# Four PSUM banks as tiles of one bank each, in a windowed attention with a maxout layer computed by a Strassen scheme

## The chip, the cores and the metric

The kernel runs on one core of a Trainium2 chip. The metric is the device time of one execution in microseconds (us): the median of several runs, and beside it one execution that the hardware profiler recorded. TensorE is called PE here, its weight loads PEld, VectorE DVE, ScalarE ACT, GpSimd POOL, and SyncE, which issues the DMAs, SP.

## What is computed

Eight batches of eight heads attend over 576 positions, each query to 32 keys: the 32 before it, or every fourth of the last 128. The result, 4608 rows of 512, goes through a layer that takes the maximum of three products and multiplies it by a fourth matrix. All is float32.

```python
# attention: B, H, S, D = 8, 8, 576, 64; window 32, dilation 4
mask_plain = (rel >= 0) & (rel < window)
mask_dil = (rel >= 0) & (rel < window * dilation) & (rel % dilation == 0)
scores = np.where(masks, scale * q @ k.T, -1e9)
attn = np.exp(scores - scores.max(-1)); attn /= attn.sum(-1) + 1e-09
x = (attn @ v).transpose(0, 2, 1, 3).reshape(4608, 512)
# maxout: w1, w2, w3 are 512 x 768, w_out is 768 x 512
h = np.maximum(np.maximum(x @ w1, x @ w2), x @ w3)
out = h @ w_out
```

## The kernel before

Every float32 operand of the layer is split into a high and a low part that PE multiplies fast, so one product is three: high by high, high by low, low by high.

The rows are worked on in tiles: three plain ones of 512 rows (tiles 0 to 2, `plain`, line 1193) and four of 768 rows by a Strassen scheme (tiles 3 to 6, `fast`, line 1292). In a plain tile each of the 18 weight blocks gives 12 matmuls of 512 columns (L1227) into one bank, and DVE or ACT takes the running maximum into `hf`. In a Strassen tile the weights are taken in nine items of two blocks each, and an item is seven products P1 to P7 of six matmuls of 384 columns (L1396) instead of eight. P1, P6, P7 and P4 accumulate one after the other in the bank `top`, P5 and P3 in `mid`, P2 in `side`. Between them the bank is read: `copied` (line 1409) copies it to SBUF as `s1`, `s5` or `u2`, and `result` (line 1415) adds bank and copy and takes the maximum into `hf`. The products stand in an order of their own, `order` (lines 1377 to 1381): items follow each other by 7, so that P4 of an item comes after P1 and P5 of the next.

At the end of a tile, `down_part` (line 1118) multiplies `hf` by the fourth matrix in blocks of 128 rows: ACT casts the high part `h`, POOL or DVE makes the low part, PE runs 18 matmuls (L1149) into one bank, ACT copies it to `o`, and SP stores `o`. In a Strassen tile the first block is opened before the last P4.

Attention runs beside this in units of one batch and two heads. The first eight (`early`, line 565) hold scores in two neighbouring banks (`bb`) and values in two single banks and one pair of neighbouring ones; their result goes to `xs`, the input of tiles 0 and 1. The later ones (`attention`, line 837) use four single banks and write `raw`, from which the Strassen tiles make their operands.

For the Strassen weights, `sums_of` (line 1049) makes sums and differences of the weight blocks on POOL and DVE, splits them, and stores them to DRAM (`kept_a`, `kept_b`; L1085); each Strassen tile loads them again (L1357).

PSUM has eight banks. Banks 0 to 5 are three tiles `pair_0` to `pair_2` of two banks each (line 394), banks 6 and 7 the tiles `ffn_0` and `ffn_1`. `ALLOWED` (line 397) says which a buffer may take: early attention and the weights' scratch `cp` any of 0 to 5, later attention 0 to 3, a plain tile 6 and 7, a Strassen tile 4 to 7.

All work is given as steps with costs, dependences and buffers to a planner (`Plan`, line 117), which simulates the engines, picks for each engine the next step by due time, gives out the banks (`banks`, line 175: the bank that is free earliest, and of those one whose neighbour is in use), and so fixes each engine's order of instructions. Semaphores between the engines are set afterwards by the framework from the tiles that the instructions read and write. The layer's own products are chained by `prev` and keep their order; attention goes between them. PE runs filler matmuls (L1572) until the first layer product.

Of the kernel before, what the change touches and what calls it, by code (L numbers as in the profile page):

```python
# [8 lines left out]
F32 = mybir.dt.float32  # L9
# [321 lines left out]
def tile_dilated_window_attention__then__maxout_ffn(  # L331
# [16 lines left out]
    ps = ctx.enter_context(tc.tile_pool(name="ps", bufs=1, space=bass.MemoryType.PSUM))  # L348
# [21 lines left out]
    plan = Plan()  # L370
# [20 lines left out]
    KEPT["sa"] = [flat[0][:, 10752 + 2048 * i : 12800 + 2048 * i] for i in range(3)]  # L391
    KEPT["sb"] = [flat[0][:, 16896:18432], *(flat[1][:, 1536 * i : 1536 * i + 1536] for i in range(3))]

    pairs = [ps.tile([128, 2, 512], F32, name=f"pair_{i}") for i in range(3)]
    BANKS = [x[:, i] for x in pairs for i in range(2)]
    BANKS += [ps.tile([128, 512], F32, name=f"ffn_{i}") for i in range(2)]
    ALLOWED = {"b": range(6), "late": range(4), "ffn": (6, 7), "fast": range(4, 8)}

    def buf(tag, name, shape=None, dtype=None):
        if tag == "bb":  # L400
            b = Buf([x for x in pairs for _ in range(2)], "b", 8, None, None, name)
            b.width, b.allowed = 2, range(0, 6, 2)
            return b
        if tag in ALLOWED:
            b = Buf(BANKS, "b", 8, None, None, name)
            b.allowed = ALLOWED[tag]
            return b
        if tag in KEPT:
            return Buf(KEPT[tag], tag, len(KEPT[tag]), None, None, name)
        n, sh, dt = SIZES[tag]  # L410
        return Buf(big if tag in ("h", "wd") else work, tag, n, shape or sh, dtype or dt, name)

    def copy(eng, dst, src):
        if eng == "act":
            nc.scalar.copy(dst, src)  # L415
        elif eng == "pool":
            nc.gpsimd.tensor_scalar(dst, src, 1.0, 1.0, ALU.mult, ALU.mult)
        else:
            nc.vector.tensor_copy(dst, src)
# [22 lines left out]
    def tt(eng, dst, a, b, op):  # L442
        (nc.vector if eng == "dve" else nc.gpsimd).tensor_tensor(dst, a, b, op=op)  # L443


    def act(n, psum=True):
        return (0.155 if psum else 0.195) + 0.00084 * n

    def dve(n):
        return 0.15 + 0.00105 * n  # L450
# [4 lines left out]
    def pool1(n):  # L455
        return 0.22 + 0.00093 * n

    def pool(n):
        return 0.13 + 0.00238 * n
# [3 lines left out]
    DOWN = [*((f, 0, DM) for f in range(NF - 1)), (NF - 1, 0, 256), (NF - 1, 256, 256)]  # L463
    NW = NWU + len(DOWN)
    wdn = [buf("wd", f"wdn{f}") for f in range(NF)]

    def weight(j, before):

        up = j < NWU
        f, n0, n = (None, 0, 512) if up else DOWN[j - NWU]  # L470
        tag = "wd" if n == 512 else "o"
        st = buf(tag, f"st{j}", [128, 2 * n], F32)
        res = [] if up else [wdn[f]]

        def part(z):
            if up:
                return wup[:, j, z]
            return wdn[f].t[:, z, n0 : n0 + n]

        cb, cp = buf("tmp", f"c{j}"), buf("b", f"cp{j}")  # L480

        def high():
# [559 lines left out]
    ITEMS = [(f, g) for f in range(0, NF, 2) for g in range(3)]  # L1042
# [3 lines left out]

    summed = []

    def sums_of(f, g):

        i = ITEMS.index((f, g))
        j1, j2 = 3 * f + g, 3 * f + 3 + g
        c1, c2, s12, s34 = (buf("tmp", f"{x}_{i}") for x in ("c1", "c2", "s12", "s34"))
        n = 512
        a, z = slice(0, 256), slice(256, 512)

        def both(j, c):
            return plan.add(
                {"pool": pool(n), "dve": dve(n)},
                lambda e: tt(e, c.t, wup[:, j, 0].bitcast(F32), wup[:, j, 1].bitcast(F32), ALU.add),  # L1060
                [*w_of[j][:2], *before],
                [c],
            )

        before = summed[-2:]

        def made(dst, dc, x, xc, y, yc, op, deps):
            return plan.add(
                {"pool": pool(256), "dve": dve(256)},
                lambda e: tt(e, dst.t[:, dc], x.t[:, xc], y.t[:, yc], op),  # L1070
                deps,
                list(dict.fromkeys((dst, x, y))),
            )

        f1, f2 = both(j1, c1), both(j2, c2)
        t1 = made(s12, a, c2, a, c2, z, ALU.add, [f2])
        t3 = made(s34, a, c1, a, c2, a, ALU.subtract, [f1, f2])
        t2 = made(s12, z, s12, a, c1, a, ALU.subtract, [t1, f1])
        t4 = made(s34, z, c1, z, s12, z, ALU.subtract, [t2, f1])
        out = []  # L1080

        def store(dst, src, deps, bufs, n):
            out.append(
                plan.add(
                    {"sp": 0.5}, lambda _: nc.sync.dma_start(out=dst, in_=src()), deps, bufs, nbytes=512 * n  # L1085
                )
            )

        for s, h, deps, dst in ((s12, c1, [t2, t3, t4], kept_a[i][:, 1024:]), (s34, c2, [t1, t3, t4], kept_b[i])):
            hi = plan.add(  # L1090
                {"act": act(n, False), "pool": pool1(n)},
                lambda e, s=s, h=h: copy(e, h.t.bitcast(F32R), s.t),
                deps,
                [s, h],
            )
            lo = plan.add(
                {"pool": pool(n), "dve": dve(n)},
                lambda e, s=s, h=h: tt(e, s.t.bitcast(F32R), s.t, h.t, ALU.subtract),
                [hi],
                [s, h],  # L1100
            )
            summed.append(lo)
            store(dst[:, :512], lambda h=h: h.t, [hi], [h], 512)
            store(dst[:, 512:1024], lambda s=s: s.t, [lo], [s], 512)
        store(kept_a[i][:, :1024], lambda: wup[:, j1].rearrange("p z n -> p (z n)").bitcast(F32), w_of[j1][:2], [], 1024)
        store(
            kept_b[i][:, 1024:].rearrange("p (z n) -> p z n", z=2),
            lambda: wup[:, j2, :, 256:].bitcast(F32),
            w_of[j2][:2],
            [],  # L1110
            512,
        )
        return out
# [178 lines left out]
    def fast(t0, prev):  # L1292
# [58 lines left out]
        for i in range(len(ITEMS)):  # L1351
# [5 lines left out]
                    lambda _, b=b, src=src: nc.sync.dma_start(out=b.t.bitcast(F32), in_=src),  # L1357
# [17 lines left out]
            "P4": (1, 1024, 256, "T4"),  # L1375
        }
        order = sorted(
            (7 * i + (2 if k == "P2" and not i else at), k, i)
            for i in range(len(ITEMS))
            for k, at in (("P1", 0), ("P5", 1), ("P6", 3), ("P2", 4), ("P3", 5), ("P7", 6), ("P4", 9))  # L1380
        )
# [66 lines left out]
        for _, k, i in order:  # L1448
            f, g = ITEMS[i]
            x = state[i]  # L1450
            name = f"{t0}_{i}"
# [21 lines left out]
            else:  # L1473
                if i == len(ITEMS) - 1:
                    down, stored = opened()
                    for h in range(4):
                        prev = down(h, prev)
                st = product(k, i, x["top"], False, [x["read"]])
                result(f + 1, g, 0, x["top"], None, [st])
        for h in range(4, NF):  # L1480
            prev = down(h, prev)
        stored(((0, t0 + n, 128),), prev, False)
        for c in (n + 128, n + 256, 0, 128, 256):
            parts = {f: [*done[f, int(c >= n)]] for f in range(NF)}
            down, stored = down_part(f"{t0}_{c}", c, "fast", ((0, 6),), parts, prev)
            for f in range(NF):
                prev = down(f, prev)
# [6 lines left out]
    for j in range(NW):  # L1494
        plan.lead = 0.0 if j < NWU else WEIGHT_LEAD
        w_of[j] = weight(j, w_of[j - 1][2] if j else None)
    plan.kind, plan.lead = "s", 0.0
    kept = [sums_of(*x) for x in ITEMS]
    prev = None

    def units(us):

        nonlocal loaded
        new = []
        for u in us:
            plan.lead = UNIT_LEAD * (NPAIR - 1 - u % NPAIR)
            *x, loaded = attention(u, loaded)
            new.append(x)

        def scores(_):  # L1510

            for rows in (64, 32):
                for x in new:
                    x[0](rows)

        s = plan.add(
            {"pe": SCORES * len(us) + 0.29}, scores, [d for x in new for d in x[1]], [b for x in new for b in x[2]]
        )
        made = []
        for u, x in zip(us, new):  # L1520
            plan.lead = UNIT_LEAD * (NPAIR - 1 - u % NPAIR)
            made.append(x[3](s))

        def values(_):

            for x in made:
                x[0]()

        s = plan.add(
            {"pe": VALUES * len(us) + 0.18}, values, [d for x in made for d in x[1]], [b for x in made for b in x[2]]  # L1530
        )
        for x in made:
            x[3](s)
# [16 lines left out]
    for n in TILES:  # L1550
        plan.kind = "a"
        while HALF * 2 * (u // NPAIR) < t0 + n:
            for p in range(NPAIR):
                if u < EARLY_UNITS:
                    plan.lead = UNIT_LEAD * (NPAIR - 1 - p)
                    x_of.extend(early(u // NPAIR, p if u >= NPAIR else PORDER[p]))
                else:
                    n_u = 1 if u < ALONE else 2
                    if u < ALONE or u % 2 == 0:
                        units(range(u, u + n_u))  # L1560
                u += 1
        if n == PLAIN:
            prev = plain(t0, prev)
        else:
            prev = fast(t0, prev)
        t0 += n
# [75 lines left out]
```

## Time and profile before

| | |
|---|---|
| median of 3 runs | 701.11 us (699.19 to 701.18) |
| the profiled execution | 699.94 us, of which its span 698.2 us |
| PE busy in the span | 659.8 us (95%) |
| DVE, ACT, POOL busy | 436.4, 291.2, 261.2 us |
| mean DMA rate | 197 GB/s |

The span is what the profile shows from the first instruction to the last; the rest of the time lies around it. An engine's busy time is the union of its instructions, so overlapping matmuls count once. The chain that ended last is 82% PE, 11% DVE and 3% ACT. The stages in order of time: attention and weights up to about 31 us, tile 0 to 118, tile 1 to 198, tile 2 to 274, and the four Strassen tiles from there to the end, each with its down blocks behind its products.

### The profile page before, as it was taken

The page shows a single profiled execution, that of the slowest core. Times are in us where ns is not written, and L with a number is a line of the kernel's source. Part 1 is how long each engine was busy: PE and PEld are TensorE (multiplying, and loading weights), DVE is VectorE, ACT ScalarE, POOL GpSimd, SP SyncE. Part 2 cuts the span into 40 slices and gives each one's busy share as a digit, 9 for nine tenths or more (in the row PEclk, how much of TensorE's full clock was granted, in tenths as well). Part 3 has the DMA queues.
Part 4 walks back from the last instruction along what each step waited for, and adds up shares of the span by engine and source line. Part 5 has one row for each costly group of instructions (what it writes and reads, how often), then busy time and mean ns, then how long its engine had stood idle before and what let it go on. Part 6 is the DMA issues. An engine that isn't in the chain of part 4 may idle for free.

```text
span 698.2 us, 15903 instructions
## 1 busy us (share of the span) xinstructions
PE 659.8 (95%) x6243; PEld 564.3 (81%) x6243; DVE 436.4 (63%) x1257; ACT 291.2 (42%) x890; POOL 261.2 (37%) x293
## 2 busy tenths in 40 slices
PE   7899989999999999999989999989999988999986
PEld 4577868888788888999957999976999966999865
DVE  5789874788877875988798477672144470234400
ACT  3465555645656555435643642244212242221131
POOL 5465679888894362103262202043000052000031
PEclk9999999999999999999999999999999999999999
DMA  9899636455374169787824477641476641565001
GB/s 345 311 353 365 270 98 220 167 198 201 99 232 143 40 236 350 275 299 263 303 101 165 138 246 249 243 170 46 137 242 238 222 156 60 177 222 203 1 31 60
DMA packets 39723, 137.48 MB, mean 197 GB/s; under 512 B 4064, under 2 KB 10720, under 8 KB 35040
## 3 DMA queue, kind: packets, MB, share of 16 engines
q1 hardware_dynamic: 39648, 136.46, 55.9%
q8 instruction: 49, 0.80, 0.5%
q14 instruction: 26, 0.21, 0.1%
HBM read 110.49 MB, written 25.95 MB: 195 GB/s over the span
## 4 chain that ended last, share of the span: by engine, by line
PE 82%; DVE 11%; ACT 3%; issue 2%; POOL 1%; ACTq 0%; POOLq 0%; DVEq 0%
PE ffn L1227 21%; PE pair L1396 20%; PE pair L1149 13%; PE ffn L1396 13%; PE ffn L1149 6%; PE pair L871 3%; PE pair L1031 3%; DVE hf L443 2%; DVE s L443 2%; ACT s L415 2%; ACT o L415 1%; DVE xs L443 1%; PE ffn L1572 1%; PE pair L617 1%; DVE wup L443 1%
## 5 line engine op out<-in xcount | busy, mean ns | idle before, releaser
L1227 PE MATMUL ffn<-xs,wup 128*128 128x512 f32 x648 | 151.4, 392 | 0.4 <-ACT hf L415 0.4
L443 POOL TENSOR_TENSOR h<-hf,h 128x768 fp32r<-128x768 f32 (+2 forms) x36 | 66.4, 1844 | 206.1 <-ACT h L415 196.3
L1227 PEld LDWEIGHTS ffn<-xs,wup 128*128 128x128 f32 x648 | 120.5, 188 | 26.5 <-ACT hf L415 0.8
L975 DVE STREAM_TRANSPOSE PT<-W 32x256 f32<-32x256 f32 (+2 forms) x288 | 109.5, 380 | 14.9 <-POOL W L443 6.0
L1149 PE MATMUL pair<-wdn,h 128*128 128x512 f32 x378 | 94.0, 398 | 15.9 <-ACT o L415 11.2
L1396 PE MATMUL pair<-wup 128*128 128x384 f32 x522 | 103.4, 336 | 0.7 <-ACT s L415 0.3
L1149 PEld LDWEIGHTS pair<-wdn,h 128*128 128x128 f32 x378 | 69.0, 188 | 38.7 <-ACT o L415 18.0
L1396 PE MATMUL ffn<-wup 128*128 128x384 f32 x504 | 99.3, 335 | 0.0
L921 ACT ACTIVATE W<-W,mx 128x96 f32<-128x96 f32 (+2 forms) x240 | 86.6, 364 | 18.9 <-DVE mx L909 18.5
L1396 PEld LDWEIGHTS pair<-wup 128*128 128x128 f32 x522 | 91.2, 188 | 2.8 <-ACT s L415 2.3
L1396 PEld LDWEIGHTS ffn<-wup 128*128 128x128 f32 x504 | 88.2, 188 | 0.8 <-DVE s L443 0.4
L1149 PE MATMUL ffn<-wdn,h 128*128 128x512 f32 x270 | 69.2, 407 | 1.1 <-POOL h L443 0.4
L443 POOL TENSOR_TENSOR W<-W,sm 128x768 f32<-128x768 f32 (+2 forms) x48 | 46.6, 976 | 48.5 <-DVE sm L950 48.1
L1396 PE MATMUL pair<-wup,xs 128*128 128x384 f32 x288 | 60.0, 343 | 2.8 <-ACT s L415 1.9
L1149 PEld LDWEIGHTS ffn<-wdn,h 128*128 128x128 f32 x270 | 50.7, 193 | 14.7 <-POOL h L443 1.2
L415 ACT CAST h<-hf 128x768 fp32r<-128x768 f32 (+4 forms) x43 | 30.7, 730 | 69.3 <-PE pair L1149 37.4
L1396 PEld LDWEIGHTS pair<-wup,xs 128*128 128x128 f32 x288 | 49.7, 188 | 8.6 <-ACT s L415 8.2
L415 ACT COPY s<-pair 128x384 f32<-128x384 f32 x36 | 17.2, 479 | 86.9 <-DVE s L443 55.6
L909 DVE CUSTOM_DVE_ANT_0 W<-pair,steps 128x96 f32<-128x96 f32 (+1 forms) x216 | 41.4, 253 | 7.1 <-PE pair L871 6.7
L921 ACT ACTIVATION_READ_ACCUMULATOR W<-W,mx 128x1 f32 (+1 forms) x240 | 45.4, 189 | 0.0
L945 POOL TENSOR_TENSOR sm<-sm,small_c 128x8 f32<-128x8 f32 (+2 forms) x48 | 11.6, 247 | 82.2 <-ACT W L921 81.7
L443 DVE TENSOR_TENSOR hf<-ffn,hf 128x512 f32<-128x512 f32 (+1 forms) x42 | 28.1, 668 | 19.7 <-PE ffn L1227 17.0
(119 smaller groups left out, 826.8 us busy)
## 6 DMA issues: line engine op xcount, KB each, us to landing
wup<-kept_a SPq DMA_DIRECT2D x36, 1024.0 KB, 6.2
xs<-kept_b SPq DMA_DIRECT2D x27, 768.0 KB, 4.2
st<-in_w_up_dram SPq DMA_DIRECT2D x18, 512.0 KB, 6.0
out_dram<-o SPq DMA_DIRECT2D x34, 256.0 KB, 2.0
k<-in_qk_d_dram SPq DMA_DIRECT2D x12, 648.0 KB, 5.1
k<-in_qk_p_dram SPq DMA_DIRECT2D x12, 592.0 KB, 6.2
wup<-kept_b SPq DMA_DIRECT2D x9, 768.0 KB, 4.3
kept_a<-wup SPq DMA_DIRECT2D x9, 512.0 KB, 6.7
```

The source lines that it names most:

```text
L415: nc.scalar.copy(dst, src)
L443: (nc.vector if eng == "dve" else nc.gpsimd).tensor_tensor(dst, a, b, op=op)
L617: nc.tensor.matmul(half(j)[32 * r : 32 * r + nq, 64 * n : 64 * n + 64], qb.t[d, q0 : q0 + nq], kb.t[d, ko + k0 : ko + k0 + 64], start=Fals ...
L871: nc.tensor.matmul(banks[j].t[o : o + nq, 96 * m : 96 * m + nk], kb.t[d, q0 : q0 + nq], kb.t[d, k0 : k0 + nk], start=True, stop=True,)
L909: nc.vector.tensor_tensor_reduce(W.t[rows, a], banks[j].t[rows, 96 * m : 96 * m + nk], mask_of(m)[rows], -0.125, 3e38, ALU.add, ALU.min, m ...
L921: nc.scalar.activation(W.t[rows, a], W.t[rows, a], AF.Exp, bias=mx.t[rows, n : n + 1], scale=-1.0, accum_out=sm.t[rows, n : n + 1],)
L945: nc.gpsimd.tensor_tensor(d, d, eps_c[rows].broadcast_to([d.shape[0], n]), op=ALU.add)
L975: plan.add({"dve": dve(32 * n) + 0.02}, lambda _: nc.vector.transpose(dst(), src()), [*deps, blank], [W, PT])
L1031: nc.tensor.matmul(pv[z].t[64 * j : 64 * j + 64, q : q + c1 - c0], v.t[d, j, y], PT.t[d, 576 * j + 96 * x + c0 : 576 * j + 96 * x + c1], s ...
L1149: nc.tensor.matmul(bank.t, hb.t[:, hz, f], wdn[f].t[:, wz], start=(f == 0 and m == 0), stop=(f == NF - 1 and m == 2), skip_group_check=True,)
L1227: nc.tensor.matmul(bank.t, wup[:, j, wz, 128 * c : 128 * c + 128], xs[:, xz, c, first : first + n], start=(m == 0 and c == EARLY[0]), stop ...
L1396: nc.tensor.matmul(bank.t[:, :n], wb.t[:, w : w + 128], xop[o][:, xz, c], start=start and not m and not c, stop=m == 2 and c == 1, skip_gr ...
```

## The change

`pair_2` goes: banks 4 to 7, which the Strassen tiles use, become four tiles of one bank each. The wide buffers `bb` may take two pairs instead of three. Which banks a single buffer may take stays as it was. In the first item of each Strassen tile P7 is put behind P1 of the second item and P4 behind its P6. The steps of `sums_of` are given to the planner after tile 0 and depend on the last down product of that tile (`after`); the stores that copy weight blocks straight from `wup` don't.

```diff
@@ -391,15 +391,15 @@
-    pairs = [ps.tile([128, 2, 512], F32, name=f"pair_{i}") for i in range(3)]
+    pairs = [ps.tile([128, 2, 512], F32, name=f"pair_{i}") for i in range(2)]
     BANKS = [x[:, i] for x in pairs for i in range(2)]
-    BANKS += [ps.tile([128, 512], F32, name=f"ffn_{i}") for i in range(2)]
+    BANKS += [ps.tile([128, 512], F32, name=f"ffn_{i}") for i in range(4)]
     ALLOWED = {"b": range(6), "late": range(4), "ffn": (6, 7), "fast": range(4, 8)}
 
     def buf(tag, name, shape=None, dtype=None):
         if tag == "bb":
             b = Buf([x for x in pairs for _ in range(2)], "b", 8, None, None, name)
-            b.width, b.allowed = 2, range(0, 6, 2)
+            b.width, b.allowed = 2, range(0, 4, 2)
             return b
@@ -1046,7 +1046,7 @@
-    def sums_of(f, g):
+    def sums_of(f, g, after):
@@ -1062,7 +1062,7 @@
-        before = summed[-2:]
+        before = [after, *summed[-2:]]
@@ -1375,7 +1375,7 @@
         order = sorted(
-            (7 * i + (2 if k == "P2" and not i else at), k, i)
+            (7 * i + (0 if i else {"P2": -2, "P7": 1.2, "P4": 1.5}.get(k, 0)) + at, k, i)
             for i in range(len(ITEMS))
             for k, at in (("P1", 0), ("P5", 1), ("P6", 3), ("P2", 4), ("P3", 5), ("P7", 6), ("P4", 9))
         )
@@ -1494,9 +1494,7 @@
-    plan.kind, plan.lead = "s", 0.0
-    kept = [sums_of(*x) for x in ITEMS]
-    prev = None
+    prev = kept = None
@@ -1561,6 +1559,9 @@
         if n == PLAIN:
             prev = plain(t0, prev)
+            if not t0:
+                plan.kind = "s"
+                kept = [sums_of(*x, prev) for x in ITEMS]
         else:
             prev = fast(t0, prev)
```

## Rows read from the trace of the kernel before

**Rows 1.** Busy time by stretch (start:end length, PE, PEld, DVE, ACT, POOL, clock, DMA).

```profile
102.60:118.60 16.00, 16.00 (x214) 12.77 (x215) 6.92 (x49) 9.37 (x41) 15.12 (x16) 0.89 0.61 208
118.60:254.80 136.20, 134.59 (x1345) 110.25 (x1344) 106.77 (x421) 77.84 (x309) 98.36 (x116) 1.00 0.48 157
...
494.00:560.50 66.50, 65.40 (x365) 62.84 (x364) 26.67 (x49) 16.93 (x35) 2.08 (x2) 1.00 0.66 227
560.50:594.80 34.30, 29.07 (x124) 22.20 (x124) 13.67 (x14) 9.89 (x15) 13.00 (x7) 1.00 0.25 90
```

**Rows 2.** PE's waits over the span: line, releaser, us in total, times, longest.

```profile
PE pair L1149 <- ACT o L415: 11.2, 16, 0.7
PE pair L1031 <- DVE mx L909: 4.2, 2, 2.7
...
PE pair L1149 <- DVE s L443: 2.8, 3, 1.1
PE pair L1396 <- ACT s L415: 2.2, 11, 0.5
...
PE pair L1149 <- DVE hf L443: 2.0, 3, 0.7
```

**Rows 3.** Timeline around one P4, tile 5: start, us, engine, instruction, idle before.

```profile
506.69 1.20 PE L1396 MATMUL pair<-wup 128*128 128x384 f32 x6
...
507.93 0.56 DVE L443 TENSOR_TENSOR s<-pair,s 128x384 f32<-128x384 f32 x1 [0.84 <-PE pair L1396]
...
508.57 0.48 ACT L415 COPY s<-pair 128x384 f32<-128x384 f32 x1 [3.89 <-DVE s L443]
...
509.10 1.34 PE L1396 MATMUL pair<-wup,xs 128*128 128x384 f32 x6 [0.17 <-ACT s L415]
```

**Rows 4.** Pieces of the chain that ended last: start, us, what.

```profile
300.87 1.05 PE pair L1396 x6
...
308.16 1.07 PE pair L1396 x6
...
405.38 2.39 PE pair L1396 x12
...
501.35 2.37 PE pair L1396 x12
...
555.34 2.38 PE pair L1396 x12
...
656.12 2.35 PE pair L1396 x12
```

**Rows 5.** Down blocks into `ffn` and `pair`: first and last the chain, between them the timeline.

```profile
254.76 10.90 PE ffn L1149 x48
...
569.70 0.58 ACT L415 COPY o<-pair 128x512 f32<-128x512 f32 x1 [0.47 <-PE pair L1149]
...
570.34 4.37 PE L1149 MATMUL pair<-wdn,h 128*128 128x512 f32 x18 [0.68 <-ACT o L415]
...
575.38 4.39 PE pair L1149 x18
```

**Rows 6.** Timeline around the last P4 of tile 5.

```profile
562.59 2.35 PE L1149 MATMUL pair<-wdn,h 128*128 128x512 f32 x9 [1.07 <-DVE s L443]
...
564.43 2.46 POOL L443 TENSOR_TENSOR h<-hf,h 128x768 fp32r<-128x768 f32 x1 [2.79 <-DVE h L443]
...
567.31 2.35 PE L1149 MATMUL pair<-wdn,h 128*128 128x512 f32 x9 [0.65 <-DVE hf L443]
```

**Rows 7.** Timeline in tile 0's down stage: a weight sum, and PE's values.

```profile
98.21 1.94 DVE L443 TENSOR_TENSOR s<-c,s 128x256 f32<-128x256 f32 x1
...
101.49 1.08 PE L738 MATMUL pair<-PT,fv 32*64 32x64 f32 x80 [2.10 <-ACT raw L415]
```

**Rows 8.** Timeline: scores of the last early unit, and their last read.

```profile
73.03 1.02 PE L617 MATMUL pair<-fk 64*32 64x64 f32 x80
...
86.58 0.81 DVE L443 TENSOR_TENSOR W<-pair,fmx 128x640 f32<-128x640 f32 x1
```

## Prediction

> **What bounds the kernel now.** I first read the busy time by stretches. In the loop of products of the third Strassen tile PE works 65.40 of 66.50 us, and in the stretch of its down products only 29.07 of 34.30 us; the next engine, DVE, is far from full in both [rows 1]. So PE sets the time there, and what counts is every stop of PE. Then I read the list of waits for who ends these stops. The largest entry, 11.2 us in 16 stops, is a down product (L1149) that waits for ACT's copy of a finished block to `o`; next to it stand 2.8 and 2.0 us behind DVE, and 11 waits of a Strassen product (L1396) for ACT's copy to `s` [rows 2]. All four entries name `pair`, although the down products and the Strassen products use `ffn` banks as well. That is what the reader is to see: banks 4 and 5 are two halves of one tile `pair_2`, banks 6 and 7 are tiles of their own.
>
> Third, one item of the loop in order of time. P7 has written one bank of the pair when P1 of the next item starts at 506.69 for 1.20 us into the other. DVE is to read P7's bank; a product's span of 1.20 us reaches 0.16 us past the next one's start (products of six matmuls follow each other every 1.04 us), so that bank is complete at 506.85. DVE is idle for 0.84 us, yet it starts only at 507.93, released by PE, just after P1 ends (506.69 + 1.20 = 507.89). ACT's copy of P1's bank then starts at 508.57, when DVE's read of the other bank has ended (507.93 + 0.56 = 508.49), and P4, which accumulates into the bank that DVE has read, starts at 509.10, after ACT's copy of P1's bank [rows 3]. Three waits in a row, each for a bank that the waiting instruction does not touch. The control is tile 3, the first Strassen tile, where the same loop falls on other banks: the 42 matmuls of an item take 308.16 - 300.87 = 7.29 us. In the third Strassen tile the same 42 take (555.34 - 501.35) / 7 = 7.71 us [rows 4]. In the down stage it is the same: 48 matmuls into `ffn` run through in 10.90 us, 0.227 us each, while those into `pair` stop for 0.68 us before each 18, and the copy that they wait for itself began only at 569.70, behind the first products of the next block [rows 5]. I take it that waits are made per tile and not per bank.
>
> **The change, part by part.**
>
> *Banks 4 and 5 as tiles of their own.* (a) The stop before P4. There are 22 such pieces, from 405.38 to 656.12 [rows 4], each 7.71 - 7.29 = 0.42 us: 9.3 us. If only the waits of the list go, it is 2.2 us [rows 2]; I take 9.3, since the control is the same loop. What is late next: P4 needs DVE's read of P7, which could start at 506.9 and end at 507.4, while P4's turn comes at 508.77 (P5's start one product of 1.04 us after P1's, and one more); nothing waits there. (b) The 16 stops before a copy to `o`. The period of a block is 575.38 - 570.34 = 5.04 us, 18 matmuls without a stop are 18 x 0.227 = 4.09 us [rows 5], so 0.95 us each, 15.2 us; the waits alone are 11.2 us [rows 2]. I take 15.2 us. (c) The stops around the last P4, behind `s` and `hf` of DVE: 2.8 + 2.0 = 4.8 us [rows 2]; the two in the third Strassen tile are of 1.07 and 0.65 us [rows 6]. Sum 29.3 us.
>
> What is late next in (b) and (c): the low part of `h` for the second block. POOL makes it from 564.43 for 2.46 us, to 566.89 [rows 6]. PE comes to the second block after three of the nine matmuls from 567.31, at 567.99. Without the stops of 1.07 and 0.65 us and their refill (0.95 less 0.68, 0.27) it would come there about 2 us sooner, at 566.0, and want that low part for the third matmul, at 566.4: 0.5 us of waiting in each of the two tiles that also prepare operands for a next one, 1.0 us. Later blocks have a whole block (4.09 us) for ACT's cast and POOL's 2.5 us. Left: 28.3 us.
>
> *Two pairs for the wide buffers instead of three.* Each of the first eight attention units takes a whole pair twice, for scores and for values. A pair is held long: the last unit's scores start at 73.03 and are read until 86.58 + 0.81 = 87.39, 14.4 us [rows 8]. But PE has the products of tile 0 to fill with, and tile 1 starts at about 118, so these units have room. I cost it at nothing; what hides it is PE's queue of tile 0's products. Without that cover one wait is at most one hold, 14.4 us; a gain is possible too, as `cp` banks in 4 and 5 no longer wait for each other, but the one large stop of this stage in the trace, 2.10 us [rows 7], has another cause. I take 0, the side of the cover, and keep those 2 us either way for the range.
>
> *The first group's order.* P7 comes one product later (after the next P1), P4 one (after the next P6). The number of products stays, and the list has no stop of PE that an operand of this group ends [rows 2]; cost 0, and a product of slack, 1.04 us, more for P7 behind ACT's copy. What hides it: the next item's P1, which now runs in P7's place and whose weights are loaded ahead. If they came late, PE would stand for them once per tile; a product's 1.04 us in four tiles, 4 us, is the bound that I keep in the range.
>
> *Weight sums after tile 0.* Before, DVE takes up sums in the middle of tile 0's down stage, the last of them 1.94 us long at 98.21; the evacuations queue behind them, and PE's next values product stands 2.10 us until 101.49 [rows 7]. In the stretch after it the granted clock was 0.89 of full speed over 16.00 us, against 1.00 in the others [rows 1]: after PE had stood, part of the stretch ran on the lower level of 1.2 GHz, and (1 - 0.89) x 16.00 = 1.8 us of work were lost. With the sums behind tile 0 I expect both gone: 2.1 + 1.8 = 3.9 us. If something else is late there, it is 0. What the sums do later: their first step now waits for the last down product of tile 0; behind it in POOL's queue are the next units' normalisations, but the planner places the step where it is due, so I cost that wait at nothing (without this cover PE or POOL stands once for what PE runs behind its plan; the 2.10 us stop of this stage is the nearest row). POOL is busy 98.36 of 136.20 us from 118.6 to 254.8, and what moves there is less than its 15.12 us from 102.6 to 118.6 [rows 1]: 113.5 of 136.2, it fits. Moved with each sum are its four stores on SP's queue, behind tile 1's loads of attention; the reloads come with the Strassen tiles after 254, so 20 us of room are left for both. The stores straight from `wup` don't move.
>
> Sum: 28.3 + 3.9 = 32.2 us. The profiled execution took 699.94 us (its span is 698.2, the rest lies around it and stays): 667.7 us. The median of the runs, 701.11, lies 1.2 above it: **668.9 us**.
>
> **Rivals.** *The stops are a lack of banks.* The same gap in each item could mean that a product waits for a bank to come free. The Strassen tiles have four banks before and after, so all 29.3 us would stay: 701.1 us, or 697.2 with the gain of the sums. Against it: P4 accumulates into a bank that its item already holds, and the wait ends with a copy out of another bank [rows 3]. This is also the rule against the change in the Trainium skill, Perfetto Trace Analysis, "Optimization Strategy": a gap that repeats on the engine that should be full can mean too little PSUM for the next tile. By that rule the time would be the one just given; the trace speaks for sharing, not for shortage. A lack of banks is also the case in which the change doesn't do what it says.
>
> *POOL takes the stops over.* Once PE no longer waits for ACT, each block of a down stage wants its `h` 0.95 us sooner. If the cast, POOL's work on the next tile's operands and the 2.5 us for `h` [rows 6] together come too late in every block, the 15.2 us of (b) stay: 684.1 us. For it: POOL's work there stretches to 2.46 us beside DVE. Against: it is idle more than half of that stretch, 13.00 of 34.30 us busy [rows 1].
>
> *Slower: two pairs starve the early attention.* Place: the second batch's four units, whose values must be in `xs` before tile 1's products, the stretch from 118.6. Now the last of them has its values product at 101.49 [rows 7], so with some 3 us for the evacuation 14 us are left. If a single-bank buffer sits in one of the two pairs, all units go through the other, each after the one before: three holds of 14.4 us [rows 8] ahead of the last unit, 43.2 us, 29 us late: 698 us. It turns slower than before when a hold grows beyond (32.2 + 14) / 3 = 15.4 us; at 18 us it is 40 us late, 709 us. For it: single buffers may lie in any of the six banks, so they can break up both pairs. Against: the planner sees every bank and delays the single ones too.
>
> **How the numbers follow.** Forecast as summed, 662 to 676 us: 0.66. POOL takes over, to 685: 0.18. Lack of banks: 0.09, of which 0.05 at 701 (no change) and 0.04 at 697.2. Starved pairs: 0.07. Within 0.3% is about what a measurement of this kernel can tell from no change. So faster 0.66 + 0.18 + 0.04 = 0.88, same 0.05, slower 0.07. The range: below, 668.9 less the 1.0 of POOL, the 4.2 us of values behind `mx` in the list [rows 2] and six refills of 0.27 in (c), 662; above, the POOL case, 685. What is left out is 0.16 and the edge of that case.
>
> **What would show it.** Right: no wait of L1149 for `o` and of L1396 for `s`; an item's 42 matmuls in 7.3 us in the last three tiles; blocks of 4.1 to 4.2 us; no sums before tile 0's last down product, and a granted clock of 1.00 there. If the items still take 7.7 us, the sharing was not the cause; if blocks take 5 us and the waits name POOL `h`, the second rival holds; if PE stands before 118 us, the third. Wrong in size would be the prediction if a new stop of several us appears where operands of the next tile are made.

## The result

The changed kernel takes 672.23 us (median of four runs, 670.83 to 1053.36) against 700.77 us for the kernel before beside it: a ratio of 0.959, 95% interval 0.956 to 0.962. The run of 1053.36 us was disturbed, at a clock of 0.56; it is in this median but in no ratio, and the median of the other three is 671.05 us. Forecast were 668.9 us, from 662 to 685. So the time lies in the range, 3.3 us above the forecast by the first median, 2.2 by the second. The profiled execution took 673.41 us, its span 671.6 us.

The gain by parts, from the starts of the tiles in the two profiled executions:

| part | before, us | after, us | difference |
|---|---|---|---|
| to the start of tile 1 | 118.40 | 113.73 | -4.7 |
| tile 1 | 79.28 | 83.82 | +4.5 |
| tile 2 | 75.37 | 77.15 | +1.8 |
| Strassen tiles 3 to 6, to the end of the span | 425.15 | 396.90 | -28.2 |

The Strassen part gives what the forecast summed for the banks (28.3 us). That it agrees to 0.1 us is partly luck: two profiles of one kernel, the banks' edit alone (below), take 394.08 and 397.48 us for this part. The 3.9 us that the weight sums should have brought were won in tile 0 and lost again in tiles 1 and 2.

PE's waits of the kernel after (line, releaser, us in total, times, longest), against [rows 2]:

```profile
PE pair L1031 <- DVE mx L909: 6.2, 2, 3.5
...
PE ffn L1149 <- POOL h L443: 2.1, 5, 0.6
PE ffn L1227 <- DVE hf L443: 1.5, 1, 1.5
```

The four entries of [rows 2] that the argument used are gone: no wait for ACT's `o` or `s`, none of L1149 for DVE's `s` or `hf`. What grew is the values product L1031, from 4.2 to 6.2 us; its wait in tile 1 went from 1.5 to 3.5 us, the other, of 2.7, stayed. `hf` in tile 2 is new. The same stretches as [rows 1], third Strassen tile (start:end length, PE, PEld, DVE, ACT, POOL, clock, DMA share, GB/s), and pieces of the chain that ended last:

```profile
485.90:549.20 63.30, 63.30 (x368) 63.30 (x367) 25.34 (x47) 16.98 (x34) 1.28 (x1) 1.00 0.66 235
549.20:577.50 28.30, 27.67 (x122) 22.17 (x122) 16.77 (x16) 10.22 (x15) 13.42 (x7) 1.00 0.33 117
```

```profile
485.90 62.42 PE ffn L1396 x360
...
645.77 21.77 PE ffn L1149 x96
```

In the loop PE works 63.30 of 63.30 us, and 360 matmuls are one unbroken piece: 62.42 / 60 = 1.04 us for each six, 7.28 us for an item. 96 down matmuls run through at 0.227 us each, a block in 4.08 us instead of the 5.04 of [rows 5].

One thing that was said of the change doesn't hold as it stands: the sums do not wait for the last down product of tile 0. The dependence counts in the planner's simulation alone. On the chip POOL's first sum starts at 111.85 us, and the last six down products run from 112.23 to 113.89.

### The profile page after: what moved, and what is told of

The parts are those of the page before. It is cut to its first block, busy times and chain, and to the rows that moved or that the text cites. A ratio compares the mean times of both kernels' runs of the same rounds, so it can differ in the third digit from the quotient of the medians.

```text
span 671.6 us, 15958 instructions
## 1 busy us (share of the span) xinstructions
PE 648.5 (97%) x6243; PEld 567.6 (85%) x6243; DVE 438.2 (65%) x1255; ACT 294.6 (44%) x893; POOL 264.4 (39%) x292
## 4 chain that ended last, share of the span: by engine, by line
PE 79%; DVE 10%; POOL 7%; issue 3%; ACT 1%; DMA 0%; POOLq 0%; ACTq 0%; DVEq 0%
PE ffn L1396 38%; PE ffn L1149 15%; PE ffn L1227 15%; DVE wup L443 4%; PE pair L1031 3%; POOL s L443 3%; PE pair L871 3%; PE ffn L1573 2%; DVE hf L443 1%; DVE raw L443 1%; PE pair L617 1%; POOL c L443 1%; DVE xs L443 1%; POOL h L443 1%; POOL W L443 1%
## 5 line engine op out<-in xcount | busy, mean ns | idle before, releaser
L1396 PE MATMUL ffn<-wup 128*128 128x384 f32 x1026 | 187.6, 334 | 0.0
L1396 PEld LDWEIGHTS ffn<-wup 128*128 128x128 f32 x1026 | 178.5, 188 | 0.7
L1149 PE MATMUL ffn<-wdn,h 128*128 128x512 f32 x648 | 156.0, 396 | 2.1 <-POOL h L443 2.1
L1227 PE MATMUL ffn<-xs,wup 128*128 128x512 f32 x648 | 151.8, 392 | 1.5 <-DVE hf L443 1.5
L1149 PEld LDWEIGHTS ffn<-wdn,h 128*128 128x128 f32 x648 | 120.7, 189 | 30.8 <-POOL h L443 5.3
L1227 PEld LDWEIGHTS ffn<-xs,wup 128*128 128x128 f32 x648 | 120.5, 188 | 28.0 <-DVE hf L443 1.9
L1396 PE MATMUL ffn<-wup,xs 128*128 128x384 f32 x486 | 93.9, 335 | 0.0
L415 ACT COPY s<-ffn 128x384 f32<-128x384 f32 x72 | 34.5, 480 | 116.5 <-PE ffn L1396 112.5
L1396 PEld LDWEIGHTS ffn<-wup,xs 128*128 128x128 f32 x486 | 84.9, 188 | 0.5
L443 DVE TENSOR_TENSOR s<-ffn,s 128x384 f32<-128x384 f32 x48 | 26.6, 554 | 46.6 <-PE ffn L1396 45.5
L443 DVE TENSOR_TENSOR wup<-raw,wup 128x768 fp32r<-128x768 f32 x25 | 37.3, 1518 | 7.4 <-ACT wup L415 5.2
L415 ACT COPY u<-ffn 128x384 f32<-128x384 f32 x36 | 17.3, 480 | 40.4 <-PE ffn L1396 40.4
```

The costliest lines, as they stand in the source:

```text
L1149: nc.tensor.matmul(bank.t, hb.t[:, hz, f], wdn[f].t[:, wz], start=(f == 0 and m == 0), stop=(f == NF - 1 and m == 2), skip_group_check=True,)
L1227: nc.tensor.matmul(bank.t, wup[:, j, wz, 128 * c : 128 * c + 128], xs[:, xz, c, first : first + n], start=(m == 0 and c == EARLY[0]), stop ...
L1396: nc.tensor.matmul(bank.t[:, :n], wb.t[:, w : w + 128], xop[o][:, xz, c], start=start and not m and not c, stop=m == 2 and c == 1, skip_gr ...
```

## The experiments

What follows is in the order of the questions. Where a ratio stands, it is to the kernel before on the same chip, with its 95% interval; a row's line numbers can be one or two off where an edit shifts them.

**Is it the sharing?** First I gave the changed kernel its shared tile back and left all else alone.

```diff
-    BANKS += [ps.tile([128, 512], F32, name=f"ffn_{i}") for i in range(4)]
+    both = ps.tile([128, 2, 512], F32, name="both")
+    BANKS += [both[:, i] for i in range(2)]
+    BANKS += [ps.tile([128, 512], F32, name=f"ffn_{i}") for i in range(2)]
```

> The changed kernel with one thing undone: banks 4 and 5 are one tile of two banks again, so a reader of one and a writer of the other meet in the same tile; number of banks, where each product lies, and the order of the work stay those of the changed kernel. Theory (the stops come from the sharing of a tile): the Strassen part gets its stops back, 28 us by the stretch 273 to the end of both kernels, so about 700 us; the list of PE's waits shows line 1149 behind ACT's o (about 16 times 0.7 us) and the matmul rows of 1396 behind ACT's s again, and an item takes 7.7 instead of 7.28 us. Rival (there were too few banks free, or the order of the work did it): the time stays at 671 to 674 us and the waits behind ACT's o stay away.

Measured: 678.23 us, 0.968 (0.966 to 0.971). Neither theory said that: only 6 of the 28 us come back. PE's waits, and PE's timeline in the third Strassen tile (start, us, instruction, count):

```profile
PE both L1151 <- DVE s L445: 1.7, 1, 1.7
...
PE both L1151 <- ACT o L417: 1.4, 2, 0.7
```

```profile
507.61 2.24 PE L1398 MATMUL ffn<-wup 128*128 128x384 f32 x12
509.69 1.23 PE L1398 MATMUL both<-wup 128*128 128x384 f32 x6
510.76 2.24 PE L1398 MATMUL ffn<-wup 128*128 128x384 f32 x12
512.84 1.20 PE L1398 MATMUL both<-wup 128*128 128x384 f32 x6
```

The reader is to see where the products lie. 507.61 is P7 of one item and P1 of the next, 510.76 P4 and P6: all four go to `ffn`, banks 6 and 7. In [rows 3] P1 and P4 went to `pair`. An item's long-held bank (P1, P6, P7 and P4 use it, `top`) alternates with that of the next item. Before the change this pair of banks was 4 and 5 in tiles 4 to 6, and 6 and 7 in tile 3 alone, which was the prediction's control. In the changed kernel it is the other way round, but for the first item of tile 3. The planner places banks by when they come free: by its list, the changed kernel has the old placing with early sums and the new one with moved sums. The stops of `o` and `s` were therefore gone for two reasons at once, and this run took away only one.

To test the sharing alone, the banks had to be held still. Two kernels have the same order of work and the same bank for each product, `top` on 4 and 5 in tiles 4 to 6. By the planner's list the two agree step by step; they differ only in whether banks 4 and 5 are one tile. The first is the kernel before with the banks' edit alone:

```diff
-    pairs = [ps.tile([128, 2, 512], F32, name=f"pair_{i}") for i in range(3)]
+    pairs = [ps.tile([128, 2, 512], F32, name=f"pair_{i}") for i in range(2)]
-    BANKS += [ps.tile([128, 512], F32, name=f"ffn_{i}") for i in range(2)]
+    BANKS += [ps.tile([128, 512], F32, name=f"ffn_{i}") for i in range(4)]
-            b.width, b.allowed = 2, range(0, 6, 2)
+            b.width, b.allowed = 2, range(0, 4, 2)
```

> The kernel before with the banks' edit alone: four tiles of one bank for banks 4 to 7, two-bank work on two pairs instead of three; sums and first group as before. Theory: 28 us less in the Strassen part than before, about 672 to 673 us, with the first group's old order costing 0 to 1 us. If the first group's new order is needed for the gain (its old order waits for a bank once per tile), 674 to 678 us. Rival of two pairs being too few for attention: PE's waits for a pair before 273 us grow, and the time is above 676 us.

The second has only the last of these three edits, two pairs for the wide buffers:

> The kernel before with one half of the banks' edit alone: wide buffers may use two pairs instead of three, but banks 4 and 5 stay one tile. Its order of work and its banks are those of the run with the banks' edit alone (668.6 us): in tiles 4 to 6 the long-held banks of the items (P1, P6, P7, P4) alternate between 4 and 5, and the down blocks too. Only the tile's shape tells the two apart. Theory (waits are made per tile): 698 to 701 us, all 30 us of the stops are there, with line 1149 behind ACT's o 16 times. Rival (the freer choice of banks for attention, or another order, brought the gain): 668 to 673 us.

Measured: 668.59 us, 0.955 (0.952 to 0.958), for the first. Its list of PE's waits has none for ACT's `o` or `s`; of the down products only the wait for POOL's `h` is left:

```profile
PE pair L1031 <- DVE mx L909: 4.2, 2, 2.7
...
PE ffn L1149 <- POOL h L443: 1.5, 4, 0.4
```

The second takes 700.75 us, 1.000 (0.999 to 1.001), and its waits of PE are those of [rows 2]:

```profile
PE pair L1149 <- ACT o L415: 11.2, 16, 0.7
...
PE pair L1149 <- DVE s L443: 2.8, 3, 1.1
PE pair L1396 <- ACT s L415: 2.2, 11, 0.5
```

So the shape of the tile alone is worth 4.5%, some 31 us, and two pairs for the wide buffers cost nothing. This is the pair of runs that decides for waits per tile. It also decides against a lack of banks, since both have the same eight, used alike.

**Does any sharing cost, or only some?** The kernel before, no tile changed, with the choice of banks narrowed for `top` and the down blocks:

```diff
-    ALLOWED = {"b": range(6), "late": range(4), "ffn": (6, 7), "fast": range(4, 8)}
+    ALLOWED = {"b": range(6), "late": range(4), "ffn": (6, 7), "fast": range(4, 8), "top": (6, 7)}
-                x["top"] = buf("fast", f"top{name}")
+                x["top"] = buf("top", f"top{name}")
```

and "top" for "fast" in the two calls of `down_part`.

> The kernel before with no tile changed: three pairs, banks 4 and 5 one tile. Only the choice is narrowed: an item's long-held bank (top) and the down blocks of the Strassen tiles take banks 6 and 7, which were tiles of their own all along; what is short (mid, side) then takes 4 and 5. Theory (what costs is that the two long-held banks, and two blocks in turn, alternate within one tile; the short ones in a shared tile cost nothing, as tile 3 before shows): 668 to 674 us, without splitting any tile. Rival (any sharing costs, wherever it lies): the stops move to the products into mid and side and the time stays at 690 to 701 us.

Measured: 676.77 us, 0.965 (0.963 to 0.967). 24 of the 31 us come without splitting a tile, by choosing which banks share one; the time lies 3 us above what I expected. Of the waits a few around the last P4 are left:

```profile
PE ffn L1149 <- DVE hf L443: 0.7, 3, 0.2
...
PE pair L1396 <- DVE hf L443: 0.4, 2, 0.2
```

From the start of tile 3 to the end of the span it takes 398.96 us, the banks' edit alone 394.08, and 397.48 in its second profile, which has a stop of 1.5 us ahead of scores (L871): some 2 to 5 us of sharing are left there, and another 2 to 3 in tile 0 (87.7 us from its first product of L1227 to tile 1, against 85.1 and 84.5).

**What are the sums worth?** Alone, on the kernel before; and the changed kernel without that part:

```diff
-    plan.kind, plan.lead = "s", 0.0
-    kept = [sums_of(*x) for x in ITEMS]
...
+            if not t0:
+                plan.kind = "s"
+                kept = [sums_of(*x, prev) for x in ITEMS]
```

> The kernel before with the sums' move alone: they are planned once the first tile's instructions are planned; banks and first group as before. Prediction's working: 3.9 us less than before, about 697 us. Theory now: the gain of some 4.7 us in tile 0 is given back in tiles 1 and 2, so 699 to 702.5 us, within 1.5 us of before, with the crowd on POOL and a stop of 2 to 4 us near 180 us. Rival (the loss in tiles 1 and 2 needs the two pairs): about 696 us without those stops.

> The changed kernel with the weight sums planned from the start, as before the change; banks and the first group's order stay changed. Prediction's working (the sums' move gains 3.9 us): about 675 to 676 us. Theory now, from the stretches of both profiles (the move gains 4.7 us up to 114 us and loses it and 1.5 us more in tiles 1 and 2, where POOL is full and slows DVE): 669 to 672 us, within 2 us of the changed kernel; the stop of about 2 us near 100 us and the clock of 0.94 after it are back, and the stops behind DVE's mx near 180 us and hf near 236 us are gone. Rival (the sums' place doesn't matter at all and the loss in tiles 1 and 2 has to do with the banks): the same time, but with the stops near 180 and 236 us still there.

Measured: 700.72 us, 1.001 (1.000 to 1.003), for the sums' move alone, and 669.66 us, 0.956 (0.953 to 0.958), for the changed kernel without it. The move alone brings nothing: it shortens tile 0 by 5.3 us and lengthens tiles 1 and 2 by 4.9 and 0.8. In the run with early sums tile 0's stop (1.8 us) and its clock of 0.94 are back and the stop of `hf` is gone, as expected; the one near 180 us is not gone but 1.48 us. To size the move I ran three kernels on one chip, with the first group's order as the third part:

> The changed kernel itself, beside the next two on one chip, so that parts of 1 to 3 us can be told apart: 671 to 673 us.

```diff
-            (7 * i + (0 if i else {"P2": -2, "P7": 1.2, "P4": 1.5}.get(k, 0)) + at, k, i)
+            (7 * i + (2 if k == "P2" and not i else at), k, i)
```

> The changed kernel with the first group's old order; banks and sums as changed. Theory (the new order costs a stop of about 1 us ahead of line 871's scores in tile 3 and gains nothing, once each bank is a tile of its own): 1 to 1.5 us less than the changed kernel beside it, 670 to 671.5 us, without that stop near 293 us. Prediction's working (cost 0): the same time. Rival (the old order waits for a bank once per tile): 2 to 4 us more.

> The kernel before with the banks' edit alone, beside the two others: it differs from the old-first-group run by the sums' place alone. Theory (the sums' move loses what it gains, and a stop of hf in tile 2 more): 1.5 to 3 us less than that run, 668 to 669 us. Prediction's working (the sums' move gains 3.9 us): 3.9 us more than that run.

Measured: 671.63 us, 0.960 (0.958 to 0.962), for the changed kernel; 673.03 us, 0.960 (0.959 to 0.962), with the old first group; 667.66 us, 0.954 (0.951 to 0.956), with the banks alone. The first group's order changes nothing that can be measured; I had expected it to cost 1 us, for a stop ahead of scores (L871), but this stop comes and goes whatever that order is, even between two runs of one kernel (none and 1.5 us with the banks alone). The last two differ by the sums' place alone: 0.0067 of 700, some 4.7 us, by which early sums are faster; between the changed kernel and its run with early sums above it is 0.959 - 0.956, some 2 us, and there the two intervals overlap. In their profiles tile 0 (from its first L1227) lasts 84.5 us with early and 81.5 with moved sums; tile 1 79.28 and 84.18; tile 2 75.37 and 77.18.

**Where tile 1 loses it.** Its end in the kernel after, on PE, DVE and POOL:

```profile
175.97 1.21 PE L1149 MATMUL ffn<-wdn,h 128*128 128x512 f32 x4 [0.59 <-POOL h L443]
180.68 1.66 PE L1031 MATMUL pair<-PT,v 64*64 64x96 f32 x38 [3.49 <-DVE mx L909]
...
183.77 3.17 PE L1149 MATMUL ffn<-wdn,h 128*128 128x512 f32 x9
```

```profile
174.15 5.94 DVE L443 TENSOR_TENSOR xs<-raw,xs 128x768 fp32r<-128x768 f32 x3 [0.73 <-POOL xs L417]
```

```profile
174.08 1.84 POOL L443 TENSOR_TENSOR h<-hf,h 128x768 fp32r<-128x768 f32 x1
175.88 1.99 POOL L443 TENSOR_TENSOR s<-s,c 128x512 fp32r<-128x512 f32 x1
177.83 1.98 POOL L443 TENSOR_TENSOR h<-hf,h 128x768 fp32r<-128x768 f32 x1
179.77 1.44 POOL L443 TENSOR_TENSOR s<-s,c 128x512 fp32r<-128x512 f32 x1
```

PE's values product waits 3.49 us for DVE's last reads of the scores (`mx`), which stand in DVE's queue behind three adds for `xs`. These take 5.94 us while POOL goes from `h` to a sum to `h` to a sum. With early sums (the banks alone, again) the adds have less beside them, and the stop is shorter. It is not that tile 1 has many more sums: POOL works 47.9 us on them there in the kernel after, and 45.0 with early sums. What differs is what stands beside the adds at its end:

```profile
182.43 1.00 PE L1031 MATMUL pair<-PT,v 64*64 64x96 f32 x40 [1.48 <-DVE mx L909]
```

```profile
177.33 3.80 DVE L443 TENSOR_TENSOR xs<-raw,xs 128x768 fp32r<-128x768 f32 x3
```

The longer stop has a second price. The granted clock from 180 to 197.7 us, first after, then the banks alone:

```profile
180.00:197.70 17.70, 17.02 (x201) 14.37 (x202) 14.90 (x60) 7.07 (x23) 13.08 (x15) 0.84 0.55 182
```

```profile
180.00:197.70 17.70, 16.22 (x208) 13.43 (x208) 16.41 (x81) 8.57 (x35) 15.38 (x19) 1.00 0.69 218
```

Part of the first stretch ran at the lower level of 1.2 GHz, and (1 - 0.84) x 17.7 = 2.8 us of work were lost by it. The stops account for (3.49 + 0.59) - 1.48 = 2.6 us; together 5.4, enough for the 4.5 by which tile 1 grew. Two causes were possible: the sums beside DVE's adds, or PE, 4 us ahead, meeting an end that attention sets anyway. The last run takes the sums out of tile 1:

```diff
-            if not t0:
+            if t0 == PLAIN:
```

> The changed kernel with the weight sums begun a tile later still, behind the last down product of tile 1: tile 1 then runs without any sum. It starts at 112 to 114 us, as in the changed kernel. Theory (the sums' adds on POOL hold up DVE's adds for xs, and so the stop before tile 1's last values products): that stop is 1.5 us or less, tile 1 lasts about 79.3 us as with early sums, and tile 2 starts near 192 us; what it gives later is open, since tile 2 must then take all sums (more than 50 us of POOL's work), I expect stops behind hf or h there and 670 to 680 us in all. Rival (PE, 4 us ahead, meets an end that the attention's own work sets): the stop stays above 3 us, with a slower clock behind it, and tile 1 lasts 83 to 84 us.

Of this run only the time to the start of tile 2 is used. Its sums come so late that some read `wup` where the Strassen operands already lie (POOL still takes up `c<-wup` at 279.18, behind the first Strassen product at 270.48), so from tile 3 on it computes with other sums; in all it takes 680.33 us. PE's timeline at the end of tile 1:

```profile
171.28 6.99 PE L1149 MATMUL ffn<-wdn,h 128*128 128x512 f32 x30
178.20 0.94 PE L1031 MATMUL pair<-PT,v 64*64 64x96 f32 x38
...
179.86 2.33 PE L1149 MATMUL ffn<-wdn,h 128*128 128x512 f32 x9
...
191.44 7.44 PE L1227 MATMUL ffn<-xs,wup 128*128 128x512 f32 x32
```

There is no stop at all. Tile 1 starts at 114.35, about as in the kernel after, and lasts 77.09 us, less than with early sums; the first sum runs at 186.24, behind the place of the stop. PE's lead is no reason to lose it; the sums in tile 1 are. Which part of that is the slower adds is not shown by itself: without the sums the planner also orders DVE's queue another way, with reads of the scores between the adds.

**A version that beats both.** The banks alone (668.59 and 667.66 us in two runs) already do. Beside it I kept DVE from taking sums, `{"pool": pool(n)}` for `{"pool": pool(n), "dve": dve(n)}` in the three steps of `sums_of`:

> The run with the banks' edit alone (668.6 us), and the weight sums on POOL only, so that DVE takes none of them up; they are planned from the start as before. If DVE's nine sums in tile 0's down stage cause the stop of about 2 us near 99 us: that stop is gone and tile 1 starts 2 to 4 us sooner. Theory (what tile 1 gains ahead of its last values product is given back there, where DVE and POOL set the end): 667 to 670 us. Rival (the gain stays where tile 1's stop doesn't grow): 664 to 666 us. Rival 2 (POOL becomes late for h of tile 1): above 671 us, with line 1149 behind POOL's h for more than 3 us.

Measured: 667.61 us, 0.952 (0.951 to 0.954), the best of all, though not apart from the banks alone (0.952 to 0.958 and 0.951 to 0.956). The stop in tile 0 behind ACT's `raw` is gone, so DVE's sums did cause it (there are three of them in tile 0's down stage, 4.0 us in all, not nine). Tile 0 lasts 83.76 us instead of 85.09 and 84.51 in the two runs of the banks alone, tile 1 80.75 instead of 79.28, so what tile 0 won is given back:

```profile
PE ffn L1149 <- POOL h L443: 3.3, 5, 1.7
PE pair L1031 <- DVE mx L909: 2.5, 2, 2.0
```

## Why the prediction was right, and where it was not

**Waits per tile, not per bank: right.** The two kernels that differ in the tile's shape alone differ by 31 us.

**The terms (a), (b), (c) and POOL's `h`: right in size.** Their sum was 28.3 us; the Strassen part lost 28.2 in the kernel after, and 31.0 and 27.6 in the two profiles of the banks alone. An item takes 7.28 us and a block 4.08, as said. In the Strassen tiles PE waits 1.5 us for POOL's `h`, in four waits, against 0.4 before; 1.0 was forecast. The rival by which all of (b) would stay falls.

**But the gain had a second cause that the prediction did not see.** It took the banks of each product as given. An edit ahead of tile 3 can turn the rotation, as the sums' move did in the changed kernel, and the changed kernel's own rotation would have avoided most of the stops with the shared tile, too (678.23 us). The step that failed is "The control is tile 3, the first Strassen tile, where the same loop falls on other banks": what decides which tile falls on which banks was not asked.

**Two pairs, and the first group's order, at 0: right.** 1.000 (0.999 to 1.001) for the first; 0.960 against 0.960 for the second. The bound of 14.4 us did not come in.

**Not counted: sharing in tile 0.** With shared tiles tile 0 lasts 87.3 to 87.7 us (before, two pairs only, other banks), with split ones 84.5 to 85.4 (the runs with early sums on any engine). The prediction noted that the `cp` banks in 4 and 5 would no longer wait for each other, and put it at 0; with early sums it is 2 to 3 us. With moved sums it is nothing: tile 0 lasts 82.0 us with the shared tile (the sums' move alone) and 81.5 to 82.3 with split ones. So in the kernel as changed the 0 holds, and the split and the move, measured one by one, count the same 2 to 3 us twice. Which waits make them up is not shown.

**The sums: wrong.** Forecast was a gain of 3.9 us; the runs show none for the move alone (700.72 us), and beside split banks a loss of some 2 to 5. The first half was right: the stop of [rows 7] went and tile 0 is 3 to 5 us shorter. The failed step is "113.5 of 136.2, it fits". It added up one engine over 136 us, and that sum came out (POOL is busy 109.38 us of this stretch in the kernel after). What counted was the one place in it where DVE had to finish adds for `xs` while POOL ran sums, with PE's values product waiting behind; that this product already stood for 1.5 us there in the kernel before, part of the 4.2 us of [rows 2], was the sign, and I used it only for the range. Also (1 - 0.89) x 16.00 = 1.8 us of clock was booked as the price of the stop of 2.10: in the first run of the banks alone the same product stood 1.7 us with the clock at 1.00 from 87 to 118 us, in the changed kernel with early sums 1.8 us with 0.94. How much of a short stop costs clock, these runs leave open.

By luck the two errors partly cancel: 31.4 us instead of 28.3 for the banks (700.0 - 668.6), 3.1 too little, and, from the loss of 2 to 5 us, 6 to 9 too much for the sums. That leaves 3 to 6 us; measured were 3.3, or 2.2 by the median of three.

## What to carry to other kernels

Look which banks lie in one tile before counting free banks: if the producer of one half and the reader of the other take turns, each waits for the other, and a repeating gap of PE that ends with a copy out of a bank it doesn't write is the sign. Either a split of the tile or another choice of banks cures it, and a planner that places banks by time can do the second by accident; so hold the placement still when you measure the first. And do not book work moved to an engine as free because its sum over a long stretch fits: look for the place where a queue of another engine runs beside it and PE already waits.

## What the hardware showed that was not expected

An add on DVE can stretch by most of an instruction of POOL. DVE's adds `xs<-raw,xs` at the end of tile 1 (count, shortest/median/longest ns): after, then the banks alone, then the run without sums in tile 1:

```profile
L443 DVE TENSOR_TENSOR xs<-raw,xs x4: 1156/1755/2585, 171.6 to 178.1; 128x768 fp32r<-128x768 f32 x2, 128x256 fp32r<-128x256 f32 x2
```

```profile
L443 DVE TENSOR_TENSOR xs<-raw,xs x4: 948/1124/2049, 174.3 to 179.1; 128x768 fp32r<-128x768 f32 x2, 128x256 fp32r<-128x256 f32 x2
```

```profile
L443 DVE TENSOR_TENSOR xs<-raw,xs x4: 414/688/2257, 172.3 to 176.2; 128x768 fp32r<-128x768 f32 x2, 128x256 fp32r<-128x256 f32 x2
```

The longest, 2.59 us, began at 174.15, just behind POOL's `h` (174.08 to 175.92), and ended 0.8 us after it; POOL's next sum began at 175.88 and took 1.99 us for a shape that elsewhere took it 1.28. Here they look as if they take turns rather than share: 1.84 us of `h` and 0.95 for such an add at its fastest make about the 2.66 us from the first start to the second end. The Trainium skill, SBUF — State Buffer, "Who interferes with whom", says that a DVE instruction with two inputs in SBUF contends with a GpSimd instruction that reads SBUF, over a port pair that they share under an exclusive lock. The traces agree; a small add took 0.41 us in the run without sums and up to 2.05 beside POOL.

The clock fell behind each stop of 3.5 us in tile 1 that a profile here shows (0.81 to 0.90 from 180 to 197.7 us, in five profiles with sums planned behind tile 0), and behind none of the stops of about 1.5 us there (1.00, in the kernel before and five profiles with early sums). With the sums on POOL alone the stop there is 2.0 us, and the clock fell too:

```profile
180.00:197.70 17.70, 16.41 (x201) 13.95 (x202) 15.21 (x71) 7.47 (x26) 14.01 (x17) 0.90 0.57 177
```
